# A mixture-of-experts kernel on one core: the second layer of expert 0's last four blocks as seven half-size products, with a redrawn order table

## The chip, the core and the metric

The kernel runs on one core of a Trainium2 chip. The metric is the device time of one execution in microseconds (us); lower is better. The engines are named as the profile names them: PE (TensorE matrix products), PEld (the loading of its weights), DVE (VectorE), ACT (ScalarE), POOL (GpSimd) and SP (SyncE, which here only starts transfers).

## The reference

Two parts stand one behind the other. The first is a small attention step for 8 batches, 8 heads, 512 rows and 32 state rows of width 64. Its output has 8 x (512 + 32) = 4352 rows of width 512, and these are the tokens of the second part, a dense mixture of 8 experts whose weights come from a Sinkhorn iteration:

```python
def _attn_ref(x, state):                       # B,H,S,Ns,D = 8,8,512,32,64
    scores = scale * x @ state.T;  a = softmax(scores);   xread = a @ state
    scores2 = scale * state @ x.T; a2 = softmax(scores2); sread = a2 @ x
    return concatenate([xread, sread], axis=2)

def _moe_ref(x, w_gate, w1, w2):               # 4352 rows, D = 512, E = 8, F = 1024
    P = exp(x @ w_gate - max)
    for _ in range(8):
        P /= P.sum(1, keepdims=True) + 1e-09
        P /= P.sum(0, keepdims=True) + 1e-09
        P *= N / E
    for e in range(E):
        h = maximum(x @ w1[e], 0.0)
        out += P[:, e:e + 1] * (h @ w2[e])
```

Every expert works on every token, so there are 8 x 9 pieces of work: per expert eight blocks of 512 tokens (one for each batch's `xread`) and a ninth block of 256 tokens (all `sread` rows).

## The kernel before

**Two stages.** The first stage holds the attention, the gate, the Sinkhorn iteration, all of expert 0 and the head of expert 1. It is written as a graph of some 740 small operations (`op(...)`): each has the engines it may run on with their costs, the operations that it needs, and the buffers that it takes. The order in which they are issued, and the engine of each, stand in a table written out by hand, `PLAN`: "435P" issues operation 435 on PE. `issue` walks that table. Engines run their instructions strictly in the order of issue, and wait on semaphores for what they need. The second stage, from expert 1 on, is a plain loop over (expert, block), in which `layer2` of one piece alternates with `layer1` of the next. Weights come in by DMA from the POOL queue, transposes by DMA go through the SP queue, results leave through SP and ACT.

**First layer.** `hidden_mul` (line 889) multiplies 128 of the 1024 hidden rows into a PSUM bank `hps` of 512 columns with two products (for blocks of batches, through the product V of state and w1, projected into `v_ps` by `project_ops`). Line 897 records these matmuls. ACT or DVE clips the result at 0 and writes float16.

**Second layer, expert 0.** For each 128 tokens of a block eight products of 512 columns run into a bank `yps` (line 935), and ACT or DVE copies it into the float32 accumulator `acc`. So a block of 512 tokens has 32 products of 512 columns, the block of 256 tokens has 16. Expert 0's rows are weighted with `Pmat` later, when Sinkhorn is through (`weigh`).

**Second layer, experts 1 to 7.** `layer2` uses Strassen's scheme in Winograd's form: with the hidden block as a 2 x 2 matrix of quarters (token half by hidden half) and w2 as another, seven quarter products do the work of eight. Each is 2 x 4 matmuls of 256 columns (line 334). It needs four sums of the hidden quarters (`sums`, lines 281 to 284, into the tile `sm` and in place in `Hm`) and four of the weights' (the tile `T`, line 965 for expert 1). The products go into four separate PSUM tiles, A, E, B0 and B1. Each of B0 and B1 is "marked" once by a product with the identity (`seed`, `Bseed`), so that later products and copies may add to it.

**Attention.** For each of 16 units DVE transposes the scores (line 628), finds maxima (631, 640), subtracts (`subA`, line 648), sums (666), normalizes and transposes back (674); ACT takes exponentials (652, 656); POOL normalizes (`normB`, line 662, and `normA`, line 670). The scores' PSUM tile of two banks comes from the pool `pair`, of which there is one.

**Sinkhorn.** Eight rounds of `rownorm` on DVE (lines 829 to 833), a product with ones on PE (`csb`, line 846) and `colnorm` on DVE (lines 839 to 841).

Of the kernel before, what the change touches and what calls it, by code (L numbers as in the profile page):

```python
# [9 lines left out]
FP32 = mybir.dt.float32  # L10
# [7 lines left out]
46V 62P 50H 51G 61A 71V 63P 60A 52G 64V 11G 72V 73A 80P 65V 12G 435P 401P 66A 81V 13H 79P 14G 82V 436A 88V  # L18
437A 404P 83A 67V 402A 137H 403A 89V 96H 97P 100P 84V 406A 68V 90A 98A 15G 85V 69P 86P 53G 405A 99V 87V 70A
103P 101A 102A 91V 409P 16H 92G 413P 104V 407P 410A 411P 105V 111A 438P 120P 414V 408A 419P 421P 106V 415P  # L20
112V 138S 121V 74V 439A 412A 422V 113V 417P 107A 54G 440A 75G 122V 432P 429P 123V 370V 420A 469P 128A 418A
416A 17G 108V 140P 124A 125V 423P 426P 471A 433P 114A 148V 93S 129V 430P 149V 172H 424P 76S 434A 115V 470A
109G 130V 139S 110V 126G 141V 131A 427P 18G 127V 142V 428V 431A 445P 143V 132V 94P 150A 95V 77P 425A 156P 116G
447P 151V 133V 78V 449P 446A 443P 441P 144A 455P 164V 152G 448A 117S 19H 450V 157V 444A 165V 173S 442A 451P
456A 166A 134S 20G 452A 453P 463P 158V 472P 207H 145V 175P 159V 183V 184V 457P 31G 146G 454A 176V 473A 160A
464P 185A 174S 460P 458P 461P 465A 147V 161V 21G 153S 177V 191P 47P 162G 474A 118P 167V 459A 154P 462A 178V
163V 135P 49A 168G 199V 22H 48V 179A 466P 136A 352P 475P 200V 192V 201A 193V 119V 467P 476A 194V 23G 195A 485P
202V 208S 210P 180V 169S 155A 218V 356P 353A 481P 357V 468A 487P 219V 24G 489P 181G 186V 211V 242H 486A 482A
477P 490V 488A 483P 479P 220A 170P 478A 503P 187G 480A 484V 171A 203G 196V 537P 209S 25H 212V 226P 197G 504A
505A 506P 213V 500P 182V 198V 26G 234V 221V 507A 222V 204S 188S 491P 27G 538A 227V 539A 501P 497P 502A 508A  # L30
492P 235V 243S 228V 244S 214A 229V 511P 215V 236A 523P 230A 498P 494P 216G 245P 495P 515P 512V 499A 277H 231V
524A 493A 517P 246V 253V 223S 496A 247V 521P 516A 237V 254V 519P 509P 522V 518A 248V 513P 232G 189P 520A 255A
205P 510V 224P 514V 540P 28H 278S 261P 249A 190V 269V 29G 225A 270V 262V 531P 534P 206V 238G 250V 532P 256V
358P 271A 535P 217V 541A 533A 233V 542A 312H 279S 263V 272V 536A 354P 280P 528P 543P 529P 525P 288V 289V 251G
555P 264V 281V 265A 282V 239S 257V 526P 359A 266V 544A 530V 556A 545P 355A 547P 549P 273G 553P 527A 546V 571P
313S 290A 548A 283V 605P 550A 554V 296P 267G 606V 304V 572A 305V 240P 573A 557P 284A 607A 558A 551P 297V 552A
568P 360P 258S 241V 285V 30G 291V 306A 559P 562P 574P 298V 252V 315P 299V 286V 569P 576A 268V 323V 563P 575A
274S 300A 560P 570A 292G 316V 361A 561A 581P 564A 307V 565P 362P 324V 317V 301V 325A 302G 566P 363V 582A 326V
579P 587P 583P 287V 314S 588V 591P 567A 580A 639P 608P 584A 592A 347H 303V 331P 577P 348G 641V 640A 610A 609A
339V 293S 589P 585P 275P 332V 259P 578A 327G 586A 260A 590A 294P 340V 308G 333V 341A 593P 309S 318V 319A 334V  # L40
295V 364P 594P 276V 328S 625P 619P 342V 595A 335A 365A 599P 320V 602P 343V 336V 600P 337V 603P 626A 321G 322V
329P 310P 350G 344S 601A 349G 311A 620V 345P 338V 346V 604V 366P 596P 330A 368P 369V 351G 597P 367A 371V 611P
372P 598A 695H 615P 617P 373V 612V 374P 375V 613P 614V 616A 623P 618A 621P 696H 711H 376A 705P 377V 642P 624A
622A 706A 707A 630P 643V 697V 708P 644A 378P 379V 631P 710A 627P 698V 380V 647P 632A 709A 636P 628P 381P 633P
699V 648V 637P 382V 634P 657P 629A 638A 383V 700V 653P 658A 655P 384P 651P 635A 701V 654A 725P 385V 723P 386V
702V 656A 726A 716P 652A 724A 717A 645P 659P 649P 714P 646A 650A 660A 387P 721P 715A 712P 727P 687P 722A 388V
728A 688A 667P 713A 664P 389V 390P 703V 665P 668P 391V 673P 674A 392V 661P 670P 669A 729V 393P 671P 394V 666A
662P 672A 677P 395V 718P 663A 678A 679P 675P 683P 719A 681P 720V 680A 676A 685P 396P 684A 682A 397V 686A 692P
704V 689P 693P 690P 730P 398V 694A 399P 733P 731V 691A 732A 735A 734A 400V
# [68 lines left out]
def kernel(  # L118
# [144 lines left out]
    def layer1(e, bi):  # L263
# [6 lines left out]
        for j in range(NJ):  # L270
            for i in range(2):
                fb = i * NJ + j
                hps = bank([128, S], FP32, "hps", "h")
# [46 lines left out]
    def layer2(e, bi, n):  # L320
# [30 lines left out]
        def seed(i):  # L351
            bb = bank([128, 2, DH], FP32, "Bseed", "B%d" % i)
            nc.tensor.matmul(bb.rearrange("p c d -> p (c d)"), identh, aT[:, 0, 0], start=True, stop=True)
            seeds.append(bb)

        if not n:
            for k, eng in enumerate(("DVE", "ACT", "DVE", "POOL")):
                weigh(k, eng)
        product(A, h(0, 0), w2h[:, :NJ, :DH], True)
        if not n:  # L360
            seed(0)
        Bb = seeds[n % 2]
        nc.scalar.copy(out=Bb[:, :nk], in_=A[:, :nk])  # L363
        yield
        product(Eb, s(0), T[:, 0], True)
        if not n:
            seed(1)
# [199 lines left out]
    for b in range(B):  # L567
# [30 lines left out]
        for q in range(NQ):  # L598
# [62 lines left out]
            def normB(eng, E2=E2, rrec=rrec):  # L661
                engines[eng].tensor_scalar(out=E2.tile, in0=E2.tile, scalar1=rrec.tile, scalar2=None,  # L662
                                           op0=ALU.mult)
# [59 lines left out]
            n2 = op(r(3), {"DVE": (0.10, 0.25)}, biasB, [m2], [nsB], [nmB])  # L723
# [5 lines left out]
            f2 = op(r(6), {"DVE": (0.16, 0.26)}, recB, [e2], [rrec], [rowsum])  # L729
            f2 = op(r(6), {"DVE": (0.35, 0.48), "POOL": (1.56, 1.70)} if POOLB else {"DVE": (0.35, 0.48)}, normB, [f2], [], [E2, rrec])  # L730

# [80 lines left out]
    op((30.0,), {"DVE": (0.2, 0.3)}, lambda _: nc.vector.memset(ones128, 1.0))  # L812
# [8 lines left out]
    c = sk({"PE": (0.18, 0.45)}, lambda: nc.tensor.matmul(gb.tile, ones128[0:1, :], sm_["gm"]), [c], takes=[gb])  # L821
# [34 lines left out]
    def project_ops(e, b, rank):  # L856
# [4 lines left out]
        for f in range(F // 512):  # L861
# [13 lines left out]
            t = op(rank, {"PE": (0.236, 0.52)}, mul, stT_ready + w1_ready(e, f) + ([t] if f else []), ps + ([] if f else [V]), [V] if f else [])  # L875
# [27 lines left out]

    h_ready = []
    for bi in range(len(blocks)):
# [4 lines left out]
        deps = deps + h_ready  # L910
        hT, h_ready = [], []
        part("H%d" % bi)
        for fb in range(NFB):
# [9 lines left out]
            t = op((due_e(bi) + 0.05 * 13.7 * fb,), {"PE": (0.44, 0.62)}, mul, deps, [ps, h], held)  # L923
# [3 lines left out]
        for tk in range(tn // 128):  # L927
# [3 lines left out]
            for half in range(2):  # L931
# [7 lines left out]
                last = op((due_e(bi) + 13.7 * (0.4 + 0.075 * (2 * tk + half)),), {"PE": (0.87, 1.04)}, mul,  # L939
# [9 lines left out]
    pools1 = {}  # L949

    def change(_):
        actx.close()
        tpool.append(ctx.enter_context(tc.tile_pool(name="moe_t", bufs=2)))
        pools1["h"] = ctx.enter_context(tc.tile_pool(name="hidden", bufs=2))

    part("H10")
    room = op((due_1,), {"HOST": (0.0, 0.0)}, change, gates + su_ready)

    def sums_w(i, g):
        w2h, T = wslots[1][1].tile, tsum[1]  # L960
        b11, b12 = w2h[:, :NJ, :DH], w2h[:, :NJ, DH:]
        b21, b22 = w2h[:, NJ:, :DH], w2h[:, NJ:, DH:]
        p, q = ((b12, b11), (b22, T[:, 0]), (b22, b12), (b21, T[:, 1]))[i]
        jj = ds(g * (NJ // 2), NJ // 2)
        nc.vector.tensor_sub(T[:, i, jj], p[:, jj], q[:, jj])

    def make_t(_):
        tsum[1] = tpool[0].tile([128, 4, NJ, DH], FP16, name="T", tag="T")

    tdone = op((due_1, 1), {"HOST": (0.0, 0.0)}, make_t, [room] + w2_ready(1))  # L970
    for i in range(4):
        for g in range(2):
            tdone = op((due_1, 1), {"DVE": (0.40, 0.50)}, lambda _, i=i, g=g: sums_w(i, g), [tdone])
    tdone.goal = -0.9
# [67 lines left out]
    for i, (e, bi) in enumerate(work):  # L1042
# [11 lines left out]
        if i:  # L1054
            next(v, None)
# [54 lines left out]
```

## Time and profile before

| what | value |
|---|---|
| median of 3 runs | 753.62 us (752.93 to 754.85) |
| the profiled execution | 752.75 us, of which its span 751.0 us; the other 1.75 us lie around the span |
| PE busy | 736.0 us, 98% of the span |
| DVE, ACT, POOL busy | 617.0, 517.7, 70.8 us |
| chain that ended last | PE 92%, DVE 3%, DMA, ACT and POOL 1% each |
| mean granted TensorE clock | 0.995 |

In the tables by stretch of time each engine has its busy time and, in brackets, its number of instructions; "PEclk" is the share of the TensorE clock that was granted. A timeline line has start, duration, engine, line of the program, operation, tiles (out<-in), shape and number; in square brackets stands the idle time before it and who ended it. Matmuls are pipelined, so the duration of a group includes the way of the last one through the array.

### The profile page before, as it was taken

The numbers are of one execution on the slowest core, as the hardware profiler recorded it, in microseconds if no ns is written. First come the engines' busy times: TensorE is split into PE (matmuls) and PEld (weight loads), VectorE is DVE, ScalarE is ACT, GpSimd is POOL, SyncE is SP. The second block draws the span as 40 slices with busy tenths as digits, with TensorE's granted clock in tenths as the row PEclk, the third lists the DMA queues.
The fourth block names the chain that finished last, engine by engine and source line by source line (L and its number), as shares of the span: only waits on it lengthen the run. The fifth ranks groups of instructions, "written<-read, shape, count | busy, mean of one in ns | idle before, by whom it ended". The sixth has DMA issues, their size and how long they took to land.

```text
span 751.0 us, 16151 instructions
## 1 busy us (share of the span) xinstructions
PE 736.0 (98%) x6517; PEld 502.2 (67%) x6517; DVE 617.0 (82%) x1529; ACT 517.7 (69%) x1014; POOL 70.8 (9%) x81
## 2 busy tenths in 40 slices
PE   5999999999999999999999999999999999999997
PEld 3444445666777777776776767776777767767776
DVE  5899989877888789788888788887897888887885
ACT  6876856799876766667666766667666676667662
POOL 4674410200010000100000000100001000000000
PEclk9899999999999999999999999999999999999999
DMA  9997560600033000700007000330007000002234
GB/s 179 140 134 131 82 99 1 109 6 1 1 61 53 2 1 2 113 1 2 1 2 112 2 1 1 58 57 1 1 2 112 2 1 2 1 31 94 103 113 141
DMA packets 51323, 36.71 MB, mean 49 GB/s; under 512 B 25392, under 2 KB 43824, under 8 KB 51248
## 3 DMA queue, kind: packets, MB, share of 16 engines
q0 software_dynamic: 22272, 20.97, 18.5%
q1 hardware_dynamic: 27744, 14.18, 7.6%
q8 instruction: 51, 0.84, 0.5%
q10 hardware_dynamic: 1232, 0.52, 0.3%
q14 instruction: 24, 0.20, 0.1%
HBM read 42.48 MB, written 8.91 MB: 68 GB/s over the span
## 4 chain that ended last, share of the span: by engine, by line
PE 92%; DVE 3%; DMA 1%; ACT 1%; POOL 1%; issue 0%; SPq 0%; POOLq 0%; DVEq 0%; ACTq 0%
PE hps L255 28%; PE Bseed L334 20%; PE A L334 14%; PE E L334 14%; PE yps L935 6%; PE hps L897 4%; PE v_ps L235 4%; DMA xT<-x_nat 1%; DMA x_nat<-in_x_dram 1%; PE y L312 0%; PE v_ps L870 0%; POOL a L670 0%; ACT Hm L275 0%; DVE acc L348 0%; POOL E L662 0%; PE su_ps L758 0%
## 5 line engine op out<-in xcount | busy, mean ns | idle before, releaser
L275 ACT ACTIVATE Hm<-hps 128x512 f16<-128x512 f32 (+1 forms) x496 | 265.8, 577 | 130.5 <-PE hps L255 128.1
L255 PE MATMUL hps<-aT,V 128*128 128x512 f16 x880 | 230.6, 379 | 0.0
L334 PEld LDWEIGHTS <-Hm 128*128 128x128 f16 x1888 | 181.6, 98 | 71.3 <-issue 15.9
L348 DVE SCALAR_TENSOR_TENSOR acc<-Bseed,Pmat,acc 128x256 f32<-128x256 f32 x354 | 155.0, 477 | 9.8 <-PE Bseed L334 6.9
L334 PEld LDWEIGHTS <-sm 128*128 128x128 f16 x1416 | 138.3, 98 | 34.5 <-issue 0.3
L334 PE MATMUL A<-w2h,Hm 128*128 128x256 f16 x944 | 123.7, 273 | 0.0
L334 PE MATMUL Bseed<-T,Hm 128*128 128x256 f16 x944 | 123.3, 273 | 0.0
L255 PEld LDWEIGHTS <-V 128*128 128x128 f16 x880 | 86.1, 98 | 50.8
L348 DVE SCALAR_TENSOR_TENSOR acc<-E,Pmat,acc 128x256 f32<-128x256 f32 x236 | 103.2, 476 | 13.8 <-PE E L334 13.5
L281 DVE TENSOR_TENSOR sm<-Hm 128x512 f16<-128x512 f16 (+1 forms) x122 | 50.1, 411 | 60.4 <-ACT Hm L275 60.2
L243 ACT CAST V<-v_ps 128x512 f16<-128x512 f32 x144 | 74.2, 612 | 0.0
L348 DVE SCALAR_TENSOR_TENSOR acc<-A,Pmat,acc 128x256 f32<-128x256 f32 x118 | 51.9, 479 | 17.9 <-PE A L334 17.6
L935 PE MATMUL yps<-w2h,hT 128*128 128x512 f16 x272 | 64.1, 379 | 0.1
L334 PE MATMUL E<-w2h,sm 128*128 128x256 f16 x472 | 61.7, 273 | 0.0
L334 PE MATMUL E<-T,sm 128*128 128x256 f16 x472 | 61.6, 273 | 0.0
L334 PE MATMUL Bseed<-T,sm 128*128 128x256 f16 x472 | 61.5, 272 | 0.0
L363 ACT COPY Bseed<-A 128x512 f32<-128x512 f32 (+1 forms) x62 | 34.1, 550 | 37.9 <-PE A L334 35.3
L282 DVE TENSOR_TENSOR Hm<-Hm 128x512 f16<-128x512 f16 (+1 forms) x122 | 50.3, 412 | 4.2
L284 DVE TENSOR_TENSOR sm<-Hm,sm 128x512 f16<-128x512 f16 (+1 forms) x122 | 50.2, 412 | 4.2
L283 DVE TENSOR_TENSOR sm<-sm,Hm 128x512 f16<-128x512 f16 (+1 forms) x122 | 49.4, 405 | 0.0
L194 POOL DMA_DIRECT2D w1h<-in_moe_w_dram x12 | 8.5, 714 | 396.9 <-PE hps L255 396.5
L935 PEld LDWEIGHTS <-hT 128*128 128x128 f16 x272 | 25.4, 99 | 28.9 <-issue 1.8
(127 smaller groups left out, 617.7 us busy)
## 6 DMA issues: line engine op xcount, KB each, us to landing
w1h<-in_moe_w_dram POOLq DMA_DIRECT2D x16, 512.0 KB, 7.0
w2h<-in_moe_w_dram POOLq DMA_DIRECT2D x16, 512.0 KB, 8.4
out_dram<-acc SPq DMA_DIRECT2D x32, 256.0 KB, 2.5
x_nat<-in_x_dram POOLq DMA_DIRECT2D x16, 256.0 KB, 5.6
st_st<-in_state_dram ACTq DMA_DIRECT2D x1, 256.0 KB, 4.9
st_st<-in_state_dram SPq DMA_DIRECT2D x1, 256.0 KB, 4.2
ETs<-E SPq DMA_TRANSPOSE x16, 4.3
out_dram<-acc SPq DMA_DIRECT2D x4, 64.0 KB, 1.8
```

The costliest lines, as they stand in the source:

```text
L235: nc.tensor.matmul(ps[q][ds(j * Ns, Ns), :], stT[ds(r, 64), bi, q, ds((j ^ q) * Ns, Ns)], w1h[ds(r, 64), 2 * q + j // 2, cols], tile_posit ...
L243: nc.scalar.copy(out=dst, in_=src)
L255: nc.tensor.matmul(out, lhs, rhs, start=(k == 0), stop=(k == len(terms) - 1))
L275: nc.scalar.activation(out=Hm[:, i, j, :tn], in_=hps[:, :tn], func=AF.Relu)
L281: nc.vector.tensor_add(s1, a21, a22)
L282: nc.vector.tensor_sub(a21, a11, a21)
L283: nc.vector.tensor_sub(s2, s1, a11)
L284: nc.vector.tensor_sub(s4, a12, s2)
L334: nc.tensor.matmul(dst[:, c], lhs(j, c), rhs[:, j], start=first and c == 0 and j == 0, stop=(j == NJ - 1), skip_group_check=True)
L348: nc.vector.scalar_tensor_tensor(out=dst, in0=src[:, c], scalar=p[:, k], in1=dst, op0=ALU.mult, op1=ALU.add)
L363: nc.scalar.copy(out=Bb[:, :nk], in_=A[:, :nk])
L935: nc.tensor.matmul(yps.tile, hT[fb].tile[:, ds(tk * 128, 128)], w2h[:, fb, :], start=(fb == 0), stop=(fb == NFB - 1))
```

## The change

The line numbers of the changed program are a little higher; its matmuls of the new scheme stand in one line of `strassen_ops`.

1. **Seven products for expert 0's blocks 5 to 8** (`SB0`). The first layer of these blocks writes the wide tile `Hm`; eight sums per block on DVE or POOL (`sums_h_ops`) and eight for the weights (`sums_w_ops(0)`; those of expert 1 may now be on POOL too) feed seven products. They use three PSUM banks: A from the common pool, and B and E as the two halves of the one `pair` tile ("BE"), which the attention no longer needs by then.
2. **The order table** has the same order as before up to about block 2, and is drawn anew from there on. It has 60 operations more. The subtraction of the maxima may be on POOL; `normB` on POOL is written as a product of two tensors.
3. **Marking of the banks.** The two `seed` products before expert 1's first pieces go; B0 is marked by being lent to a first-layer product, B1 by a projection. One seed product for the pair tile is added in expert 0.
4. **Early waits filled.** Before seven operations of the table, the last of which (the transposes into `aT_ps`, line 709) starts at 17.24 us in the trace of before, `idle` issues matmuls or transposes of the identity, 128 columns each, into the bank that the operation takes next: 50 + 3 + 3 + 18 + 8 + 9 + 2 = 93.

```diff
+IDLE = {56: 50, 63: 3, 80: 3, 414: 18, 97: 8, 100: 9, 69: 2}
+SB0 = (5, 6, 7, 8)
-def issue(ops):
+def issue(ops, idle):
     for step in PLAN:
...
+        idle(op.takes[0].tile if op.takes else None, IDLE.get(int(step[:-1]), 0))
         op.emit(ENGINES[step[-1]])
...
+                if eng == "POOL":
+                    nc.gpsimd.tensor_mul(E2.tile, E2.tile, rrec.tile.broadcast_to((128, S)))
...
-                s1 = op(r(4), {"DVE": (0.60, 0.80)}, subA, [m1], [], [eA, mxA])
+                s1 = op(r(4), {"DVE": (0.60, 0.80), "POOL": (1.05, 1.20)}, subA, [m1], [], [eA, mxA])
...
+    def sums_w_ops(e):
...
+                tg.append(op((due_1, 1), {"DVE": (0.42, 0.52), "POOL": (1.06, 1.20)}, sub,
...
+    def sums_h_ops(bi, rank, kept, Hm, sm, goal=None):
...
+            on = {"DVE": (0.15 + 0.29 * f, 0.25 + 0.29 * f), "POOL": (0.1 + 0.95 * f, 0.25 + 0.95 * f)}
...
+            pair = Slot(rings["pair"], lambda: bank([128, 2, 512], FP32, "BE", "pair"))
+            def seed(_):
+                nc.tensor.matmul(pair.tile[:, 0], identh, aT[:, 0, 0], start=True, stop=True, skip_group_check=True)
...
+        Bb = lambda: pair.tile[:, 0].rearrange("p (c d) -> p c d", c=2)
+        Eb = lambda: pair.tile[:, 1].rearrange("p (c d) -> p c d", c=2)
+        Ab = psum([128, 2, DH], FP32, "A")
...
+        p1 = product(A, h(0, 0), lambda: w2(0, 0), True, a11 + [ready], [Ab])
+        c1 = op(rank, {"ACT": (0.50, 0.66), "DVE": (0.62, 0.74)}, lambda eng: copy(eng, Bb()[:, :nk], A()[:, :nk]),
+                [p1] + st_last, [], [pair, Ab])
+        p2 = product(Eb, s(0), lambda: T(0), True, s1 + Tr[0] + [ready] + st_last)
+        e11 = put(Eb, 1, 1, [p2])
+        p3 = product(Bb, s(1), lambda: T(1), False, s2 + Tr[1] + [c1])
+        e01 = put(Bb, 0, 1, [p3])
+        p4 = product(A, h(1, 0), lambda: w2(1, 0), False, a12 + [c1])
+        put(A, 0, 0, [p4])
+        p5 = product(Bb, h(0, 1), lambda: T(2), False, s3 + Tr[2] + [e01])
+        x11 = put(Bb, 1, 1, [p5, e11], True)
+        p6 = product(Eb, s(2), lambda: w2(1, 1), False, s4 + [e11])
+        x01 = put(Eb, 0, 1, [p6, e01], True)
+        p7 = product(Bb, h(1, 1), lambda: T(3), False, a12 + s3 + Tr[3] + [x11])
+        y = put(Bb, 1, 0, [p7])
...
+        if bi in SB0:
+            h_ready = strassen_ops(bi, deps, held, Tr0)
+            continue
...
+    def idle(t, n):
+        for _ in range(n):
+            if t.dtype == FP16:
+                nc.tensor.transpose(t, identh, identh)
+            else:
+                nc.tensor.matmul(t, identh, identh, start=True, stop=True, skip_group_check=True)
...
-            seed(0)
...
-            seed(1)
+        if not i:
+            seeds += [bank([128, 2, DH], FP32, "Bseed", "B%d" % k) for k in range(2)]
+            l1 = layer1(*work[i + 1], None if i else seeds[0].rearrange("p c d -> p (c d)"))
```

Here `put` copies a product's bank into `acc`, or with `True` adds it there, and `product` issues the 4 x 2 matmuls of one product (4 x 1 in the block of 256 tokens). The diff is cut to what the text below speaks of.

More of the change, by code (lines that the diff above doesn't have):

```diff
@@ L22 @@
[L22 to L26, printed above, removed]
@@ L349, in add @@
                                                op0=ALU.mult, op1=ALU.add)
[L351 to L354, printed above, removed]
         if not n:
-            for k, eng in enumerate(("DVE", "ACT", "DVE", "POOL")):
+            for k, eng in ((2, "DVE"), (3, "POOL"), (0, "DVE")):
                 weigh(k, eng)
         product(A, h(0, 0), w2h[:, :NJ, :DH], True)
+        Bb = seeds[n % 2]
         if not n:
-            seed(0)
-        Bb = seeds[n % 2]
+            yield
         nc.scalar.copy(out=Bb[:, :nk], in_=A[:, :nk])
+        if not n:
+            weigh(1, "ACT")
         yield
         product(Eb, s(0), T[:, 0], True)
-        if not n:
-            seed(1)
         add(Eb, 1, 1)
@@ L661, in normB @@
             def normB(eng, E2=E2, rrec=rrec):
-                engines[eng].tensor_scalar(out=E2.tile, in0=E2.tile, scalar1=rrec.tile, scalar2=None,
-                                           op0=ALU.mult)
+                if eng == "POOL":
+                    nc.gpsimd.tensor_mul(E2.tile, E2.tile, rrec.tile.broadcast_to((128, S)))
+                else:
+                    nc.vector.tensor_scalar(out=E2.tile, in0=E2.tile, scalar1=rrec.tile, scalar2=None, op0=ALU.mult)
             def sumA(_, eA=eA, sA=sA, rA=rA):
@@ L728 @@
                 m0.group = m2.group = e2.group = ps
-            f2 = op(r(6), {"DVE": (0.16, 0.26)}, recB, [e2], [rrec], [rowsum])
-            f2 = op(r(6), {"DVE": (0.35, 0.48), "POOL": (1.56, 1.70)} if POOLB else {"DVE": (0.35, 0.48)}, normB, [f2], [], [E2, rrec])
+            f2 = op(r(6), {"DVE": (0.09, 0.20)}, recB, [e2], [rrec], [rowsum])
+            f2 = op(r(6), {"DVE": (0.28, 0.41), "POOL": (1.05, 1.20)} if POOLB else {"DVE": (0.28, 0.41)}, normB, [f2], [], [E2, rrec])
             pe = psum([128, NSC, 128], FP16, "ET_ps")
@@ L811 @@
     part("ones")
[L812 removed]
+    ones = op((30.0,), {"DVE": (0.1, 0.25)}, lambda _: nc.vector.memset(ones128, 1.0))
     part("K")
@@ L820 @@
     gb = psum([128, 1], FP32, "gm_ps")
-    c = sk({"PE": (0.18, 0.45)}, lambda: nc.tensor.matmul(gb.tile, ones128[0:1, :], sm_["gm"]), [c], takes=[gb])
+    c = sk({"PE": (0.18, 0.45)}, lambda: nc.tensor.matmul(gb.tile, ones128[0:1, :], sm_["gm"]), [c, ones], takes=[gb])
     c = sk({"DVE": (0.12, 0.25)}, lambda: nc.vector.tensor_copy(out=tile_of("nm", [128, 1]), in_=gb.tile),
@@ L902, in hidden_deps, with change, quarters @@
         return su_ready + w1_ready(e), []
+    pools1 = {}
+    def change(_):
+        actx.close()
+        tpool.append(ctx.enter_context(tc.tile_pool(name="moe_t", bufs=2)))
+        pools1["h"] = ctx.enter_context(tc.tile_pool(name="hidden", bufs=2))
+    part("H10")
+    room = op((due_1,), {"HOST": (0.0, 0.0)}, change, gates + su_ready)
+    def quarters(e, T):
+        w2h = wslots[e][1].tile
+        b11, b12 = w2h[:, :NJ, :DH], w2h[:, :NJ, DH:]
+        b21, b22 = w2h[:, NJ:, :DH], w2h[:, NJ:, DH:]
+        return ((b12, b11), (b22, T[:, 0]), (b22, b12), (b21, T[:, 1]))
@@ new lines, in sums_w_ops, with make_t, sub @@
+    def sums_w_ops(e):
+        def make_t(_):
+            tsum[e] = tpool[0].tile([128, 4, NJ, DH], FP16, name="T", tag="T")
+        part("T%d" % e)
+        got = op((due_1, 1), {"HOST": (0.0, 0.0)}, make_t, [room] + w2_ready(e))
+        done = []
+        for g in range(2):
+            tg = []
+            for i in range(4):
+                def sub(eng, i=i, g=g):
+                    p, q = quarters(e, tsum[e])[i]
+                    jj = ds(g * (NJ // 2), NJ // 2)
+                    engines[eng].tensor_sub(tsum[e][:, i, jj], p[:, jj], q[:, jj])
+                tg.append(op((due_1, 1), {"DVE": (0.42, 0.52), "POOL": (1.06, 1.20)}, sub,
+                             [got] + tg[:1] * (i == 1) + tg[1:2] * (i == 3)))
+                if e:
+                    tg[-1].goal = -0.9
+            done.append(tg)
+        return [[done[0][i], done[1][i]] for i in range(4)]
@@ L946 @@
             op((due_e(bi) + 13.7 * (0.4 + 0.075 * (2 * tk + 1)),), EVICT32, keep, [last], [], [yps]).goal = -0.5
[L949 to L974, printed above, removed]
+    sums_w_ops(1)
     for bi in range(2):
@@ L1055 @@
             next(v, None)
+        if not i:
+            seeds += [bank([128, 2, DH], FP32, "Bseed", "B%d" % k) for k in range(2)]
         l2 = layer2(e, bi, i)
-        l1 = layer1(*work[i + 1]) if i + 1 < len(work) and work[i + 1] not in hid else iter(())
+        l1 = iter(())
+        if i + 1 < len(work) and work[i + 1] not in hid:
+            l1 = layer1(*work[i + 1], None if i else seeds[0].rearrange("p c d -> p (c d)"))
+        if not i:
+            next(l2)
+            next(l1)
         for k in range(7):
```

200 lines of the change are left out of this document (150 added, 50 removed).

## The prediction

> **What bounds the kernel now.** I read the busy time by stretch first, then PE's timeline in the first 25 us, the chain of waits, and last the timelines of DVE and POOL.
>
> ```profile
> 0.00:16.00 16.00, 7.28 (x96) 5.36 (x97) 8.27 (x21) 9.01 (x17) 7.51 (x15) 1.00 1.13 174
> 16.00:24.00 8.00, 7.72 (x53) 3.32 (x54) 6.61 (x14) 6.43 (x15) 2.33 (x2) 0.58 1.27 180
> 24.00:100.00 76.00, 74.47 (x855) 35.47 (x853) 70.26 (x158) 58.01 (x133) 41.57 (x39) 1.00 0.80 117
> 100.00:140.00 40.00, 39.73 (x257) 21.13 (x255) 35.19 (x95) 25.25 (x52) 3.80 (x4) 1.00 0.19 31
> 140.00:751.00 611.00, 606.80 (x5263) 436.92 (x5260) 496.66 (x1243) 418.99 (x802) 15.55 (x22) 1.00 0.17 37
> ```
>
> The columns are stretch, length, then PE, PEld, DVE, ACT and POOL with their counts, the granted clock, DMA share and GB/s. From 24 us on PE is idle for 1.5 us up to 100 and 0.3 us up to 140: its work is the time. DVE has 92% (70.26 of 76) and 88% (35.19 of 40) there, so it is close behind. Behind 140 us the change alters nothing but the two marks.
>
> ```profile
> 7.68 1.91 PE L492 MATMUL stT_ps<-identh,st_in 128*128 128x128 f16 x16
> ...
> 14.63 0.62 PE L578 MATMUL xT_ps<-identh,x_nat 128*128 128x128 f16 x8
> 16.00 1.03 PE L578 MATMUL xT_ps<-identh,x_nat 128*128 128x128 f16 x8 [0.76 <-DMA x_nat<-in_x_dram]
> 17.24 1.21 PE L709 MATMUL aT_ps<-identh,a 128*128 128x128 f16 x8 [0.20 <-DVE a L670]
> ...
> 18.86 3.57 PE L897 MATMUL hps<-aT,V 128*128 128x512 f16 x8
> ...
> 22.98 1.90 PE L897 MATMUL hps<-aT,V 128*128 128x512 f16 x8
> ```
>
> The same eight transposes take 0.62 us at 14.63 and 1.03 us at 16.00, the same eight products 3.57 and 1.90 us: PE ran at half speed from 16 to nearly 23 us, as the 0.58 of the second row says, after a stretch with many small waits.
>
> ```profile
> 130.74 3.47 PE yps L935 x16
> ...
> 149.41 0.87 PE A L334 x8
> ```
>
> The chain gives the prices of both schemes: 16 products of 512 columns cost 3.47 us (0.217 each), a Strassen product of 8 x 256 columns 0.87 us.
>
> **The change, part by part.** The sum is made against the profiled execution, 752.75 us (span 751.0 and 1.75 around it), 0.87 below the median; the median is what I predict, so 0.87 is added at the end.
>
> (1) Products. A block of 512 tokens goes from 32 x 0.217 = 6.94 to 7 x 0.87 = 6.09 us, -0.85; the block of 256 has half, -0.42. Together 3 x 0.85 + 0.42 = -3.0 us on PE, which sets the end.
>
> (2) Marks. Two products of 512 columns go, one comes: -0.2.
>
> (3) Clock. 50 fills of 128 columns at the half-speed price (1.91 / 16, about 0.11 with its tail) are 5.4 us, and lie in the 6.9 us in which PE waits for the first x; they cost nothing. The other 43 at full speed (0.62 / 8, at most 0.08) are 3 us in waits that the timeline has between 11 and 17.5 us (0.28, 0.34, 0.50, 0.76, 0.20: 2.1 us): 0 to +1, I take +0.2, since a faster PE waits longer. If the clock then holds, the hps group saves 1.67, the transposes 0.4 and 0.6, the small groups between about 0.3: -3.0. The ends are 0 (it falls as before) and 0.42 x 8 = -3.4. DVE and ACT are at 6.61 and 6.43 of 8 there and follow a faster PE only in part: I take -2.5.
>
> (4) The shared tile. In the program as built the first matmul of the second product (into the half E of BE) waits for ACT's copy c1 into the half B, and the sixth (E) waits for DVE's addition x11 out of B: the halves are treated as one tile. In experts 1 to 7 these are separate tiles and no such wait stands in the trace. PE issues in order, so all later products and the Sinkhorn product queue behind. Prices: a result is out 0.16 us behind the last issue (273 ns for one matmul against 0.109 spacing), c1 is 0.55 to 0.60 (line 363), x11 about 0.69 (line 691, also PSUM and SBUF in, 686 ns), handing over about 0.1: 0.85 and 0.95 a block, 7.2 for four. Some first-layer products and the Sinkhorn product stand in between in the new order. Ends 1.5 and 7.2; I take +5, nearer the upper end, since most of these pairs have under 0.5 us of work between them.
>
> (5) POOL against DVE.
>
> ```profile
> 41.54 1.04 POOL L670 TENSOR_TENSOR a<-eA,rA 128x512 f16<-128x512 f32 x1 [1.59 <-DVE rA L667]
> 42.57 1.99 POOL L662 TENSOR_SCALAR E<-E,rrec 128x512 f16<-128x512 f16 x1
> ...
> 70.50 1.56 POOL L662 TENSOR_SCALAR E<-E,rrec 128x512 f16<-128x512 f16 x1
> ```
>
> ```profile
> 41.96 1.17 DVE L648 TENSOR_TENSOR eA<-eA,mxA 128x512 f32<-128x512 f32 x1
> ...
> 71.09 0.68 DVE L648 TENSOR_TENSOR eA<-eA,mxA 128x512 f32<-128x512 f32 x1
> ```
>
> A DVE operation with two SBUF tensors that starts inside a POOL product of two tensors takes 1.17 instead of 0.68 us and ends 0.55 us behind POOL's end (42.58, 43.13); the next POOL operation then takes 1.99 instead of 1.57. It happened again at 52.22 (1.17). Inside POOL's tensor-by-scalar at 70.50 DVE is not held (0.68). So two two-tensor operations exclude each other. The Trainium skill (SBUF — State Buffer, section "SBUF: two separate sides") has a rule for it that speaks against this change: DVE and GpSimd share one port pair as an exclusive lock, which a DVE operation with two SBUF inputs needs. On that rule POOL's tensor-by-scalar should have held DVE at 71.09 too; the trace does not show that, and the measurement decides.
>
> Before, POOL has 12 two-tensor operations; as built the changed kernel has 66, of which 36 are the weights' and hidden sums between some 80 and 135 us. At 1.05 each (line 670) these are 38 us in about 50. On DVE the same stage holds some 28 of the other kind: 16 of Sinkhorn, 7 hidden and 5 weight sums. Each meets POOL with about 0.75 and waits half of 1.05 on the mean: 28 x 0.75 x 0.5 = 10.5 us. DVE's slack (12% of 50, 6 us) takes about half; the rest reaches PE through Sinkhorn, sums and x11. Ends 0 and 10.5; I take +5.
>
> (6) Balance. DVE loses nine subtractions (9 x 0.75) and eleven clippings (11 x 0.68), and gains seven sums (0.42), five clippings, three copies and eight additions: about -3 us. ACT gains some 5, POOL 38. In the attention POOL is even: nine subtractions at 1.07 come, normB falls from 1.60 to about 1.07 for twelve, three normA go. So the loads that share its queue (0.8 us each) start about as before, and the SP transposes behind normB too. The most that an earlier aT can give is the 1.5 us of PE waits; at worst there is one wait more like that for xT at 52.82 us (0.90), +1. I take 0.
>
> Sum: -3.0 - 0.2 + 0.2 - 2.5 + 5 + 5 + 0 = +4.5. 752.75 + 4.5 + 0.87 = 758.1, say 758. All lower ends give -3.2 - 3.4 + 1.5 + 0 - 1.5 = -6.6, all upper ends -3.2 + 1 + 7.2 + 10.5 + 1 = +16.5.
>
> **The rivals.** *Faster, chance 0.20.* The mechanism is cover: in the stage from 85 to 135 us the redrawn table may keep enough other products ahead of each awaited one that neither c1 and x11 nor a held DVE reaches PE. It decides from the point where (4) and (5) together cost under 3 us: with 2 for both, -5.5 + 2 = -3.5, 750. For it: DVE carries 3 us less, and before only two DVE operations were held in 100 us. Against: POOL is busy three quarters of that stage, and DVE's slack is 12%.
>
> *Even, chance 0.13.* (4) and (5) cost 3 to 7: 752 to 755.5.
>
> *The fills don't hold the clock, chance 0.17.* Between 12.5 and 16 us PE stood still in many small waits and the clock fell; a faster PE waits more, and the fills must cover just that. Then (3) gives 0 and the sum is +7, 760.6; with a little more in (5), 761 to 766. The Trainium skill (TensorE: Matmul & The Clock Gate, Part 1) has the clock released by a window of about 3.4 us of activity and taken back after an idle one, with free-running windows; by it the phase of a run may decide.
>
> *The forecast, chance 0.50*, 755.9 to 765.
>
> **How the numbers follow.** A difference of 0.3%, 2.3 us, is about what can be told from no change. Faster than 751.4: the first rival, 0.20. Within: 0.13. Slower: 0.50 + 0.17 = 0.67. The range reaches from 750.5, which leaves about a tenth below, to 765.5, which leaves as much above where both large terms come near their ends.
>
> **What would show it.** Right for (1): 160 instead of 272 yps matmuls, and seven groups of 0.87 us in each of the blocks 5 to 7. For (3): the clock at 1.00 in all of 16 to 24 us and the first hps group near 1.9 us. For (4): PE idle by about 0.8 us ahead of BE groups, released by ACT BE and DVE acc. For (5): DVE two-tensor operations of 0.9 to 1.4 us instead of 0.42 (sums) and 0.44 (Pmat) between 85 and 135 us. The forecast is wrong if these have their old durations, or if PE's idle time between 85 and 140 us stays under 3 us.

## The result, and the profile after

The changed kernel takes 774.93 us (median of 4 runs, 773.46 to 775.79) against 753.27 for the kernel before on the same chip: ratio 1.0287, 95% interval 1.0270 to 1.0303, or 21.7 us slower. Forecast were 758 and a range from 750.5 to 765.5. The direction was right, the size was not. The profiled execution took 775.18 us, 772.9 of them its span.

The table by stretch, with the columns of the prediction:

```profile
0.00:16.00 16.00, 12.39 (x178) 10.63 (x179) 9.71 (x24) 10.00 (x19) 7.51 (x15) 1.00 1.14 177
16.00:24.00 8.00, 7.59 (x78) 4.12 (x76) 6.57 (x15) 7.43 (x17) 3.31 (x4) 1.00 1.41 160
24.00:100.00 76.00, 70.47 (x822) 32.89 (x821) 64.97 (x153) 56.77 (x131) 43.59 (x48) 0.93 0.95 130
100.00:140.00 40.00, 28.82 (x221) 19.91 (x220) 35.28 (x62) 15.74 (x32) 29.34 (x24) 0.96 0.05 9
140.00:160.00 20.00, 17.09 (x124) 12.11 (x124) 14.90 (x33) 11.28 (x25) 7.54 (x10) 0.91 0.00 1
160.00:772.90 612.90, 608.73 (x5278) 438.51 (x5275) 498.41 (x1248) 420.59 (x804) 18.21 (x25) 1.00 0.18 36
```

From 16 to 24 us the clock is now 1.00. But from 24 to 100 us PE is idle for 5.5 us (1.5 before), and from 100 to 140 us for 11.2 (0.3 before). DVE has 88% there, the same share as before, but with 62 instructions instead of 95. The granted clock, 1.00 everywhere behind 24 us before, is now below it in three rows; the records show five stretches of half speed, of 3.4 us each, beginning at 51.3, 88.8 (two), 109.3 and 140.0 us. That number differs from execution to execution: this one has a mean clock of 0.988, the other three have 0.993, which is some three stretches, and they take the same time (773.46 to 775.79 us). Stage two, which begins with the first A group of line 334 (now 343), starts at 157.5 us instead of 135.1. That is the whole difference; behind it the two kernels take the same within 0.6 us.

PE's timeline, the early group and some of the largest waits (in brackets the idle time before and who ended it):

```profile
18.52 1.89 PE L903 MATMUL hps<-aT,V 128*128 128x512 f16 x8 [0.22 <-ACT aT L423]
...
89.97 0.61 PE L764 MATMUL su_ps<-ETs,x_nat 128*64 128x32 f16 x16 [3.27 <-DMA ETs<-E]
105.97 0.36 PE L852 MATMUL csb_ps<-cpart,ones 128*128 128x8 f32 x2 [1.43 <-DVE cpart L839]
109.07 1.24 PE L1040 MATMUL BE<-T,sm 128*128 128x256 f16 x6 [1.64 <-DVE T L939]
114.70 1.03 PE L1040 MATMUL BE<-w2h,sm 128*128 128x256 f16 x8 [0.97 <-DVE acc L1051]
123.68 0.36 PE L852 MATMUL csb_ps<-cpart,ones 128*128 128x8 f32 x2 [2.37 <-DVE cpart L839]
131.12 1.03 PE L1040 MATMUL BE<-w2h,sm 128*128 128x256 f16 x8 [3.12 <-DVE acc L1051]
```

The first hps group takes 1.89 us instead of 3.57, as forecast. At 89.97 us PE waits for a transpose by DMA (ETs). Behind 100 us nearly all waits end with DVE: with Sinkhorn (cpart), a weight sum (T), the addition x11 (acc). The chain of waits says the same; where it was 92% PE before, between 100 and 140 us it now runs almost wholly on DVE (start, duration, engine, tile, line):

```profile
101.35 1.37 DVE T L939
103.10 0.68 DVE rsum L836
...
106.44 1.30 DVE Hm L969
107.73 1.29 DVE T L939
109.37 1.18 DVE Pmat L847
...
144.29 0.87 PE BE L1040 x8
```

The last line is the price of a product, unchanged. The others are operations that took 0.42 to 0.44 us before (rsum 0.18). Why, stands in the timelines of DVE and, below it, of POOL:

```profile
103.10 0.67 DVE L836 TENSOR_SCALAR rsum<-rsum 128x34 f32<-128x34 f32 x1
103.81 0.37 DVE L837 RECIPROCAL rsum<-rsum 128x34 f32<-128x34 f32 x1
...
106.36 1.37 DVE L969 TENSOR_TENSOR Hm<-Hm 128x512 f16<-128x512 f16 x1
```

```profile
102.40 1.33 POOL L973 TENSOR_TENSOR sm<-sm,Hm 128x512 f16<-128x512 f16 x1
103.70 1.15 POOL L939 TENSOR_TENSOR T<-w2h 128x512 f16<-128x512 f16 x1
...
106.12 1.33 POOL L939 TENSOR_TENSOR T<-w2h,T 128x512 f16<-128x512 f16 x1
```

The hidden sum of DVE at 106.36 ends 0.28 us behind POOL's sum of 106.12, and the small rsum at 103.10 ends 0.04 us behind POOL's of 102.40; the reciprocal at 103.81 is not held. Counted over DVE's timeline from 24 to 160 us (duration beyond the usual one of the same form, where over 0.15 us), 25 operations are held for 15.8 us together; before, 3 for 1.4. Of the 25, 21 stand beside POOL's sums and make 13.1 us.

### The profile page after: what moved, and what is told of

Same layout as the page of the kernel before. It is cut to its first block, busy times and chain, and to the rows that moved or that the text cites. A ratio compares the mean times of both kernels' runs of the same rounds, so it can differ in the third digit from the quotient of the medians.

```text
span 772.9 us, 16581 instructions
## 1 busy us (share of the span) xinstructions
PE 745.1 (96%) x6693; PEld 518.2 (67%) x6693; DVE 629.9 (81%) x1531; ACT 521.8 (68%) x1024; POOL 109.5 (14%) x123
## 4 chain that ended last, share of the span: by engine, by line
PE 84%; DVE 8%; DMA 3%; ACT 1%; POOL 1%; issue 1%; DVEq 0%; ACTq 0%; POOLq 0%
PE hps L261 27%; PE Bseed L343 20%; PE A L343 14%; PE E L343 13%; PE v_ps L241 4%; PE yps L1113 3%; PE hps L903 2%; DMA x_nat<-in_x_dram 1%; PE BE L1040 1%; DMA w2h<-in_moe_w_dram 1%; DMA ETs<-E 1%; DVE acc L1051 1%; DVE Pmat L838 1%; DVE Pmat L847 1%; ACT Hm L284 0%
## 5 line engine op out<-in xcount | busy, mean ns | idle before, releaser
L261 PE MATMUL hps<-aT,V 128*128 128x512 f16 x878 | 230.1, 379 | 0.0
L261 PEld LDWEIGHTS <-V 128*128 128x128 f16 x880 | 86.1, 98 | 50.5
L357 DVE SCALAR_TENSOR_TENSOR acc<-A,Pmat,acc 128x256 f32<-128x256 f32 x118 | 51.9, 479 | 16.5 <-PE A L343 16.1
L1113 PE MATMUL yps<-w2h,hT 128*128 128x512 f16 x160 | 38.8, 392 | 0.3 <-DMA w2h<-in_moe_w_dram 0.3
L903 PE MATMUL hps<-aT,V 128*128 128x512 f16 x144 | 37.1, 390 | 0.2 <-ACT aT L423 0.2
```

Of the source, the lines that this page charges most:

```text
L261: nc.tensor.matmul(out, lhs, rhs, start=(k == 0), stop=(k == len(terms) - 1))
L357: nc.vector.scalar_tensor_tensor(out=dst, in0=src[:, c], scalar=p[:, k], in1=dst, op0=ALU.mult, op1=ALU.add)
L903: nc.tensor.matmul(ps.tile[:, :tn], lhs, rhs, start=(k == 0), stop=(k == len(terms) - 1))
L1113: nc.tensor.matmul(yps.tile, hT[fb].tile[:, ds(tk * 128, 128)], w2h[:, fb, :], start=(fb == 0), stop=(fb == NFB - 1))
```

## The experiments

Times are differences to the kernel before, measured beside it on the same chip (its medians are 753.2 to 753.5). A ratio's interval reaches 0.15 to 0.3% to each side, 1 to 2 us, and the difference between two such runs is less certain still, by up to 3 us: a small one needs its trace beside it.

**The two suspects of the prediction, alone and together, and the fills.** Theory 1 was the exclusion of POOL and DVE, theory 2 the shared tile.

```diff
e1: the 36 sums in the table, e.g.   -403G 404G 650G   +403V 404V 650V
e2: -            pair = Slot(rings["pair"], lambda: bank([128, 2, 512], FP32, "BE", "pair"))
    +            pair = Slot(rings["pair"], two)      # closes the pool, opens two one-bank pools B and E
e3: both
e4: -IDLE = {56: 50, 63: 3, 80: 3, 414: 18, 97: 8, 100: 9, 69: 2}
    +IDLE = {}
```

> The changed kernel with all 36 weight and hidden sums of this stage on DVE instead of POOL, in the same order. Theory 1, two-tensor operations of POOL and DVE exclude each other: DVE gets 36 x 0.42 = 15 us more of its own work and loses the held time (Pmat and sums from 1.2-1.4 back to 0.42-0.44, the small rsum operations from 0.67 to 0.18), the waits for Sinkhorn's cpart (5.3 us) and most of those for acc (6.4) go, and with them two of the four later half-speed stretches: 774.9 - 9 to -13, so 762 to 766. Theory 2, the waits come from the one shared tile: the order and the tile stay, DVE has 15 us more to do, so no gain, 774 to 782. Theory 3, DVE was simply full: slower by up to 10.

> The changed kernel with the two halves of BE as two separate tiles of one PSUM bank each, so the second and sixth product no longer wait for c1 and x11. Theory 2 (shared tile): the waits of PE for BE released by DVE acc and ACT BE go (7.1 us, 5 times) and one or two half-speed stretches with them: 774.9 - 7 to -10, 765 to 768. Theory 1 (exclusion of POOL and DVE): the seventh product still waits for the held addition and Sinkhorn still is late, so most of the time comes back at the next wait: -1 to -4, 771 to 774.

> Both edits: sums on DVE and two tiles. If the two causes are separate and add: 774.9 - 11 - 8 = 756. If one of them hides behind the other, no better than the better of the two single edits by more than 2. If DVE is then the bound (617 us of work, 15 more in 80 to 160 us), 760 to 766 with PE waiting for DVE's own sums. A result below 752 would say that the seven products pay once both are gone.

> The changed kernel without the 93 early fills. By the prediction's term (3) the clock falls again at 16 us, hps takes 3.57 instead of 1.89, and it is slower by about 2.5: 777.4. Rival: the time won early is taken up by later waits for DMA (x, ETs) in the attention, then no difference, 774.9 within 1.

Measured: sums on DVE 771.37, +18.0 (ratio 1.0243, 1.0217 to 1.0269); two tiles 769.89, +16.5 (1.0218, 1.0189 to 1.0246); both 767.37, +14.0 (1.0192, 1.0161 to 1.0222); no fills 775.89, +22.5 (1.0303, 1.0276 to 1.0331), against +21.7 of the changed kernel. The shared tile is worth 5.2, the size that the prediction gave it, though less than the 7 to 10 of the expectation; most of it adds to the other. The sixth product no longer waits for x11, as said, but the seventh now does. PE's timeline, first in the changed kernel, then with two tiles:

```profile
131.12 1.03 PE L1040 MATMUL BE<-w2h,sm 128*128 128x256 f16 x8 [3.12 <-DVE acc L1051]
```

```profile
130.92 1.03 PE L1047 MATMUL B<-T,Hm 128*128 128x256 f16 x8 [2.86 <-DVE acc L1058]
```

The waits for additions sum to 6.4 us before 160 us in the one and 5.7 in the other. What shrank is Sinkhorn's wait (cpart, 5.3 to 2.1 us), and no half-speed stretch is left behind 100 us in that run's trace.

Moving the sums brings 3.7, not 9 to 13: in that run no DVE operation is held between 100 and 140 us, so the exclusion is gone, but DVE has 15 us of sums in its place. That is nearly the same amount: the 36 sums on POOL held DVE by 13.1 us, 0.36 each, and on DVE a sum takes 0.42. The fills are worth about 1 here, not 2.5. And with both edits 14 us remained, above both times that the expectation names (756, or 760 to 766): neither theory was the whole.

**The kernel before with single parts of the change, and late loads.**

```diff
e5: the kernel before   +IDLE = {56: 50, 63: 3, 80: 3, 404: 18, 97: 8, 100: 9, 69: 2}
e6: e5, and  -            seed(0)  -            seed(1)
    +            l1 = layer1(*work[i + 1], None if i else seeds[0].rearrange("p c d -> p (c d)"))
e7: the kernel before, table  -697V ... 704V  +697G ... 704G   (expert 1's weight sums on POOL)
e8: the changed kernel, table: 350G to behind 403G, 351G to behind 404G  (loads of expert 1's w2)
```

> The kernel before with the 93 early fills and nothing else. Term (3) of the prediction: the clock stays at 1.00 from 16 to 24 us, the first hps group takes 1.9 instead of 3.57, and the time falls by 2.5, from 753.3 to 750.8. Rival, drawn from the run without fills (only 1.0 apart from the changed kernel): DMA paces the attention, the time won before 24 us is given back in waits for x, xT and weights before 80 us, then 752.3 to 753.3.

> The kernel before with the fills and with the banks B0 and B1 marked by real products (no seed products). Terms (2) and (3): 753.3 - 2.5 - 0.4 (two products of 512 columns) = 750.4. If the fills are given back later, 752.0 to 753.0. If lending B0 to a first-layer product makes that product's bank late, up to 1 slower.

> The kernel before with expert 1's eight weight sums on POOL instead of DVE, in the same places of the order, beside Sinkhorn. If two-tensor operations of POOL and DVE exclude each other, DVE operations beside them (Pmat, the additions of sums) take 1.0 to 1.4 instead of 0.42 to 0.44, here too, in a kernel without the shared tile and without seven products, and POOL's take 1.15 or more; DVE loses 8 x 0.42 = 3.4 us of own work and up to 8 x 0.6 by holding. On the time: PE has 1.5 us or less of idle there, so -0.5 to +3, 753 to 756. If they don't exclude each other, DVE keeps 0.42 to 0.44 and the time stays.

> The changed kernel with the two loads of expert 1's w2 moved back in POOL's order, behind the first sums of expert 0's weights. If the last transposes ETs land late (89.9 us) because these loads were issued ahead of them, the wait of PE for ETs (3.3 us) shrinks to under 1 and the half-speed stretch at 88.8 goes with it: 774.9 - 3.3 - 1.6 = 770, and Sinkhorn starts 3 us earlier. Rival: something later than the transposes (the last subtraction or normalization on POOL) holds the end of the attention, then 774 to 775.

Measured: fills 752.36, -0.8 (0.9986, 0.9971 to 1.0002); fills and marks 752.09, -1.1 (0.9982, 0.9965 to 0.9999); sums on POOL 754.78, +1.6 (1.0020, 1.0005 to 1.0034); late loads 772.28, +19.1 (1.0245, 1.0216 to 1.0273).

With the fills the clock stays up, and the time is given back later. In the table by stretch of that run:

```profile
16.00:24.00 8.00, 7.56 (x78) 4.02 (x76) 6.77 (x16) 7.48 (x17) 3.75 (x3) 1.00 1.32 177
...
80.00:100.00 20.00, 18.74 (x224) 9.37 (x223) 16.12 (x37) 13.10 (x32) 8.23 (x8) 1.00 0.62 93
```

PE is idle for 1.3 us in the second row (0 before): there it waits for the last ETs, which transfers deliver and no faster PE brings. The kernel before says the same by itself. In 41 of its 68 executions here the mean clock is 0.995 or less, in 27 it is 0.997 or more, about one stretch of half speed fewer, and their mean times are 753.4 and 753.0 us.

The kernel before with POOL sums shows the exclusion without anything else of the change. DVE's timeline:

```profile
107.67 0.79 DVE L830 TENSOR_SCALAR rsum<-rsum 128x34 f32<-128x34 f32 x1
...
108.89 0.93 DVE L832 TENSOR_TENSOR Pmat<-Pmat,rsum 128x272 f32<-128x272 f32 x1
```

They are 0.18 and 0.44 us without it. The eight sums on POOL hold five DVE operations by 2.3 us in all, and spare DVE 3.4; the run is not faster.

Late loads take the wait for ETs away. In their run's table by stretch:

```profile
80.00:100.00 20.00, 19.88 (x231) 9.57 (x230) 17.78 (x41) 17.04 (x41) 14.20 (x15) 1.00 0.44 71
```

PE was busy for 16.64 of these 20 us in the changed kernel, at a clock of 0.83. There SP issued the last four ETs from 74.98 us on, the last of them at 83.16, and POOL the w2 loads at 82.81 and 85.64; the product behind the last transpose started at 89.97, 6.8 us behind its issue. With late loads the last transpose was issued at 86.78, and the products behind the last three ran without a wait from 89.64 us on. So the loads did hold the transpose up, and the wait is gone. But the attention ends no earlier: its last stretch had itself moved back by 3.6 us, and Sinkhorn's first product starts 1.8 us earlier, not 3. The 2.6 us that the run is faster, less than the 5 expected, lie within overlapping intervals.

**All three edits; then no sums at all.**

```diff
e9:  e3 and e8 together
e10: e9, and for expert 0
     -                engines[eng].tensor_add(s1, a21, a22)          (and the other sums)
     +                pass
     -        T = lambda k: tsum[0][:, k]
     +        T = lambda k: w2(k % 2, 1)
     -        s = lambda k: (lambda j, c: sm.tile[:, k, j, ds(c * 128, 128)])
     +        s = lambda k: h(k % 2, 1)
e11: e6, table: 348G (first load of expert 1's w1) to behind 321G
e12: e2 and e8 together
```

> The changed kernel with all three edits: sums on DVE, two tiles, late loads of expert 1's w2. If the three causes add: 774.9 - 7.6 - 2.7 = 764.6. If the late transposes only moved the start of a stage that DVE bounds, 766 to 767. In either case over 10 us above the kernel before remain, so that none of the three is the whole cause.

> As the run with all three edits, but expert 0's 32 hidden sums and 8 weight sums are left out (the products read plain quarters in their place), so only the seven products, their copies and additions and Sinkhorn remain. Theory: the sums themselves, wherever they run, are the price (40 x 0.42 = 17 us of DVE or as much by holding it, and PE waits for them): then the stage runs at PE's pace and the time falls by 8 to 12 below the run with sums on DVE, to 753 to 757. Rival: the turn-around product - addition - next product through PSUM is the price; then PE still waits for B and E and for Sinkhorn, and it stays above 760.

> The kernel before with fills, real marks, and the first load of expert 1's w1 moved back behind the last normalization, so that the last transposes ETs aren't behind it. If the 1.0 that the fills and marks bring now is all that they can, 752.1; if the wait for ETs that stood in the run with fills (1.3 us) goes, 750.8 to 751.5, about 0.25% under the kernel before. If the later load makes expert 1's projection wait, 753 to 754.

> The changed kernel with two tiles and late loads, sums left on POOL. Compared with the run of all three edits it gives the price of POOL's sums against DVE's with nothing else in the way, and with the run without sums the price of the sums on POOL. If edits add: 774.9 - 5.0 - 2.7 = 767.2, 2.6 above the run with sums on DVE. If holding DVE is worse than doing the sums there, 4 or more above it; if it is the same, within 1.

Measured: all three 763.16, +10.0 (1.0133, 1.0109 to 1.0156); without expert 0's sums, whose products read plain quarters instead, 752.80, -0.4 (0.9989, 0.9973 to 1.0006); e11 754.50, +1.3 (1.0013, 0.9999 to 1.0027); sums left on POOL 764.75, +11.6 (1.0158, 1.0127 to 1.0188). The third is a miss: with the load moved, expert 1's projection waits 2.25 us for w1, the last of the three cases in its expectation.

The second decides. PE in the run of all three edits:

```profile
100.00:120.00 20.00, 16.71 (x128) 11.60 (x126) 18.89 (x52) 8.89 (x18) 0.00 (x0) 0.91 0.01 3
120.00:140.00 20.00, 18.27 (x155) 13.85 (x153) 17.36 (x47) 10.37 (x25) 0.00 (x0) 1.00 0.01 2
```

and without sums:

```profile
100.00:120.00 20.00, 19.98 (x181) 15.01 (x179) 16.59 (x42) 12.85 (x26) 0.00 (x0) 1.00 0.06 10
120.00:140.00 20.00, 19.97 (x174) 15.42 (x167) 18.30 (x47) 13.13 (x29) 2.72 (x3) 1.00 0.00 1
```

Without sums PE has 0.05 us of idle time in 40, though every product, copy, addition and Sinkhorn round is still there. So behind 100 us, with the tile parted, the sums are the price: 10.4 us where DVE makes all of them (763.16 less 752.80), 12.0 where POOL makes 36 (five of these are expert 1's). The 1.6 between the two lies within their intervals. The turn-around through PSUM, the rival, costs nothing once the halves are two tiles and the sums are gone. Whether PE loses this time because a product waits for its own sums, or because a fuller DVE is late with everything else, this run does not part: without the sums both are gone.

**Why it is not below the kernel before even then.** Products, marks and fills should give 4 us here by the prediction's prices for the first two (3.0 and 0.2) and the 0.8 measured for the fills.

```diff
e13: e9, e14: e10, both with
-                    nc.gpsimd.tensor_mul(E2.tile, E2.tile, rrec.tile.broadcast_to((128, S)))
+                engines[eng].tensor_scalar(out=E2.tile, in0=E2.tile, scalar1=rrec.tile, scalar2=None, ...)
e15: e13, table  -589V 597V 626V 632V 671V 688V 710V 773V 775V 792V  +589A 597A ... 792A
```

> The run with all three edits, with normB on POOL written as tensor by scalar again, as in the kernel before. Theory: POOL's product of two tensors at 45 us holds DVE's second normalization (1.35 instead of 0.69 us), this makes the clipping hT late, PE waits 1.07 and 0.56 us at 50 us and its clock falls for 3.4 us (1.6 lost); a tensor by scalar doesn't hold DVE, so these go: 763.2 - 2 to -3 = 760 to 761. Rival: the longer operation (1.56 instead of 1.05, twelve times) delays loads and transposes in POOL's queue by as much: 763 to 764.

> The run without expert 0's sums, with the same edit of normB. Theory: the stall at 50 us and its half-speed stretch are most of what the redrawn attention loses; 752.8 - 2 to -3.5 = 749.5 to 751, the first clearly under the kernel before, which would show the gain of the seven products as priced. Rival: DMA paces the attention (waits for w2h and xT remain), 752 to 753.

> The run e13 with ten more evictions of PSUM (clippings, copies, projections) behind 85 us moved from DVE to ACT, in the same places of the order. Theory: DVE is full from 95 to 150 us (90%, with 15 us of sums) and ACT half idle; DVE loses 10 x 0.68 = 6.8 us there, and PE's waits for cpart and sm (about 6 us) shrink: 4 to 6 under e13, 755 to 757. Rival: the chain sums - product - addition has its latency in any case, then 1 or less.

Measured: 762.41, +8.9 (1.0100, 1.0078 to 1.0122); 751.66, -1.8 (0.9981, 0.9965 to 0.9996); 760.26, +6.8 (1.0085, 1.0067 to 1.0102). DVE's normalization, first in the changed kernel, then in e13:

```profile
44.57 2.00 DVE L676 TENSOR_TENSOR a<-eA,rA 128x512 f16<-128x512 f32 x1
```

```profile
44.74 0.93 DVE L674 TENSOR_TENSOR a<-eA,rA 128x512 f16<-128x512 f32 x1
```

Its usual time is 0.68. In the first, POOL's normB (44.97, 1.05 us, two tensors) stands beside it, and DVE's operation ends 0.55 us behind POOL's. The clipping behind it is late, PE waits 1.07 us at 49.3 and 0.56 at 50.6, and half speed follows from 51.3 to 54.7. In e13 and e14 the hold is down to 0.25 and the wait of 1.07 is gone. But PE then waits later, at 60 to 63 us, for an exponential (1.2 and 1.4) and for ETs (1.8 and 1.5), with a half-speed stretch there; of the 2 to 3.5 expected, 1.1 and 1.4 came, which these intervals do not tell from nothing. That the two waits make the clock fall is not shown either: the run of all three edits has the same two waits, 1.07 and 0.56 us, at 50.5 and 51.9, and its clock held. The 20 products behind them, first in the changed kernel, then in e9:

```profile
51.20 6.18 PE L1113 MATMUL yps<-w2h,hT 128*128 128x512 f16 x20
```

```profile
52.41 4.49 PE L1119 MATMUL yps<-w2h,hT 128*128 128x512 f16 x20
```

The run without sums and with this edit (e14) is just below the kernel before. Its ten executions fall into two groups: five with a mean clock of 0.999 or 1.000 took 749.6 to 751.2 us, five with 0.995 to 0.998 took 752.2 to 754.0. The ten without this edit (e10) do the same: 749.9 to 750.9 us for three, 751.7 to 754.7 for seven. At full clock the means are 3.1 and 2.9 us below the kernel before, not far from the 4 expected. This sorts the executions afterwards, so it is a hint and no test: most of what the seven products lack without their sums goes with a half-speed stretch that some executions have and others have not.

Ten evictions moved to ACT bring another 2.1, not 4 to 6, and the intervals overlap. In the traces PE's idle time from 100 to 140 us falls from 5.0 to 4.5, from 140 to 160 from 1.8 to 0; no half-speed stretch is left in that profiled execution (two of the other three have a mean clock of 0.995). So DVE's load in that stage looks like part of the price; of the rest the largest wait, 1.65 us of a Sinkhorn product at 115 us, now ends with ACT, which has taken over the evictions.

## Why the prediction was wrong, point by point

**Products and marks** (-3.0, -0.2): 160 yps products are left, and a group takes 0.87 us, as said; their -3.0 was never seen alone. The marks showed -0.3 between e5 and e6, which is too little to be told from nothing.

**Clock** (-2.5): right in the trace (1.00, and 1.89 instead of 3.57), wrong in its worth: 0.8 in each kernel. The step that failed is that DVE and ACT alone would limit what follows; in e5 a transfer does, and the wait for ETs (1.3 us) takes most of the 1.7 that are missing. That the clock, once held, may fall again later was nowhere priced: the profiled execution has five half-speed stretches behind 50 us. What they cost is open, since executions with fewer took the same time.

**Shared tile** (+5): 5.2 measured. The waits described (for x11 at the sixth product, for c1 at the second) stood in the trace and went, but the wait for x11 came back at the seventh product, and the gain came from Sinkhorn's product, which queues behind. That the size fits so well is partly luck.

**POOL against DVE** (+5, ends 0 and 10.5): the exclusion is there, and this is the term that was mis-sized. The held time was nearly right: 13.1 us beside POOL's sums against 10.5 forecast, of which 2.1 are of rsum, a form that the term had left out. The step that failed is "DVE's slack (12% of 50, 6 us) takes about half". DVE is 88% busy, but what stands behind 100 us in the chain of waits is almost one string of DVE operations, Sinkhorn's rounds and the sums, additions and copies that the next products need. The sums cost 12.0 us with most of them on POOL, and 10.4 on DVE with nothing held. So the hold as such is not the larger part: it is that these sums were given no price of their own, on whichever engine.

**Balance** (0, ends -1.5 and +1): wrong twice. The sums were counted as 2.9 us on DVE and free on POOL; by e10 and e9 they cost 10.4 even on DVE alone. (Nor does DVE's "about -3" follow from the operations counted there: at 0.68 us a clipping or copy and 0.69 an addition they come to about -0.3.) And the redrawn order issued a load just ahead of the last transpose and a second one while it was under way (2.6 by e8), and put POOL's two-tensor operations beside DVE's in the attention. I had excluded both with "the loads start about as before" and "POOL is even".

**The sum.** -3.0 - 0.2 - 0.8 + 5.2 + 12.0 + 2.6 = 15.8 of the 21.7. Another 3.6 is what the run without sums lacks of its due (-4.0 expected, -0.4 found), in the attention before 80 us. The last 2.3 is that tile and loads together bring 10.1 (21.7 less 11.6) and alone 7.8. Each of these is uncertain by 2 to 3 us. Of the 3.6 some 2.5 go with the clock (a mean of 750.3 us at full clock in e10, against its median of 752.8). What stays open is why the clock falls in some executions, and how the rest divides between the order and the transfers.

**The rivals.** None of them covered this. (The bounds of the even one, 752 to 755.5, lie a little above what its 3 to 7 us give, 751.1 to 755.1.) The range ended at 765.5 though all upper ends together gave +16.5, and even these are below what came: each term had been bounded by itself. That tile and loads together bring 2.3 more than alone is a hint that such terms raise one another; it is not shown.

**A version just ahead of both** is the kernel before with fills and marks, 752.09 us: ratio 0.9982, with 0.9999 the upper end of its interval, so barely clear of no change. The seven products do not pay in this stage in any run that makes the sums.

## What to carry to other kernels

A tensor sum moved from DVE to POOL spares DVE only what it does not take back by holding: here 0.42 us spared and 0.36 held in the changed kernel, 0.29 in the kernel before with POOL sums, and no run became faster by it. The Trainium skill (Perfetto Trace Analysis, section "Optimizing Scalar/DVE Operations") says of these two engines that moving work between them "might not help"; here it did not. And before products are traded for sums, look for the engine that makes the sums, and whether what it does in that stage is a chain that PE waits for. DVE was 88% busy from 100 to 140 us before and 87% without the sums, and PE lost 0.3 us or less; with the sums added PE lost 5.0, so the remaining eighth was no slack.

## What the runs showed of the hardware that was not expected

A DVE operation with one tensor in SBUF can be held too: rsum (34 elements, tensor by scalar) took 0.67 us beside POOL's sum instead of 0.18, E at 81.95 us 1.07 instead of 0.33 beside POOL's subtraction, while reductions, reciprocals, tensor-by-scalar operations on one element a row (nsB, 0.15 or less) and reads of PSUM kept their times. The Trainium skill (SBUF — State Buffer, section "SBUF: two separate sides") names DVE operations in a two-port mode beside those with two SBUF inputs; the trace agrees, if these small ones run in that mode, which no record shows.

A held operation ends at a fixed time behind POOL's: 0.28 us for a float16 sum, 0.30 for Pmat, 0.04 for rsum, 0.55 for the attention's operations on eA, the same in every trace here that has one. So what a hold costs can be read off POOL's end.

POOL pays as well: a float16 sum took 1.15 us in most places, also where DVE then waited for it, and 1.24 to 1.35 where a DVE operation on two tensors was still at work as it started; and its tensor-by-scalar, 1.56 alone, took 1.94 in e13 behind a DVE operation.

POOL's tensor-by-scalar in float16 did not hold DVE (0.68 us at 71.09 in the kernel before, as usual). Beside its float32 one (acc, 136.20, 1.85 us) a DVE operation of the same form took 0.92 instead of 0.49, and ended 0.60 us ahead of POOL's; why, no run here shows.

The clock fell at 51.3 us after waits of 1.07 and 0.56 us, but not in e9 after the same waits, and not between 120 and 139 us, where PE was idle for 37% of the time in waits up to 3.12 us. What decides between them no run here shows.
